# One attention score per key place modulo 128, later gate logits, and a planner that picks among sixty trial orders

## The chip, the core and the metric

The kernel runs on one core of a Trainium2 chip. The metric is device microseconds (us) of one execution, the median of several runs. A core has a matrix engine (TensorE, PE in the profile, with its weight loads shown as PEld), three engines for elementwise work (VectorE, DVE; ScalarE, ACT; GpSimd, POOL) and a queue of DMA issues (SyncE, SP). Matrix products land in PSUM, which VectorE and ScalarE read and GpSimd does not touch in this kernel.

## The reference

Attention with a window of 128 keys and a slope per head, then a mixture of eight experts whose gates are normalised in rounds over rows and columns, then one more two-layer network. Shapes: batch 4, 8 heads, 576 positions, head size 64; 2304 tokens of 512 features.

```python
def _attn_ref(q, k, v):
    window = 128
    scores = scale * np.matmul(q, k.transpose(0, 1, 3, 2))
    rel = pos[:, None] - pos[None, :]
    bias = slopes[:, None, None] * (-np.abs(rel))[None, :, :]
    mask = (rel >= 0) & (rel < window)
    scores = np.where(mask, scores + bias[None], -1000000000.0)
    scores = scores - np.max(scores, axis=-1, keepdims=True)
    attn = np.exp(scores)
    attn = attn / (np.sum(attn, axis=-1, keepdims=True) + 1e-09)
    return np.matmul(attn, v)
...
    x = _moe_ref(x=x, **moe_kwargs)      # logits, 8 rounds of row and column sums, 8 experts with relu
    return _moe2_ref(x=x, **moe2_kwargs) # x @ w_in, leaky relu, @ w_out
```

## The kernel before, in words

**Attention** walks 18 tiles of 128 tokens (`steps`, two groups of four heads each). A tile's queries can see keys of their own block and of the block before, so `scores` makes, per head, one product of 128 queries by 256 keys into PSUM (tile `s`, line 609). VectorE adds the slope times the distance, with a huge value where the window is left, and takes the minimum (line 618, 256 columns per head); ScalarE takes the exponential and its sum (line 622). `probs_T` turns the probabilities with TensorE, one 128x128 transpose per head and key block (line 690, tile `pt`), eight per group, and copies them out, half on ScalarE (line 693) and half on VectorE (line 695), as `pb`. `values` multiplies them with the values (line 708, tile `o`), and VectorE writes the weighted result into `acc` (line 716). The first tile of every second sequence (tiles 0 and 9) has no block before, so 16 tiles have two blocks. Sequences are 576 long, so tiles 4 and 13 hold the end of one and the start of the next, and tiles 5 and 14 stand 64 places into one; these four get a bias of their own (tile `dist`, line 575) and queries scaled on GpSimd (line 580).

**Inputs of the experts.** Each product of the experts is made by a scheme with seven block products, in pairs of 16-bit parts. `part` splits an input into a high part on ScalarE and a low part on GpSimd (`split`, lines 842 and 843); `sums` forms the block sums (line 894). Expert products of the first weight chunk (lines 1128 and 1244) run between attention's own products for the first pairs of tiles, and after it for the last. `logits` (line 736) makes the gate's logits of a pair of tiles, and `gate` the rounds.

**The order.** The program is written as one list, and `Plan` reorders it: `weigh` gives each instruction a cost in ns, `depend` finds what it waits for, `deadlines` works back from TensorE's products to the latest time that each instruction may end, and `order` fills the engines forward in time, at each step taking the ready instruction with the earliest latest time. `fix` ties each engine's instructions together in that order. TensorE products fall into three kinds (`mode`: by rows of 64 for the scores, by columns of 64 for values and sums, full for the rest), and `TURN` is the price of a change of kind. The order is a fixed one, made before the kernel runs.

```python
            near = t + (self.NEAR if eng != "PE" else 0)
            pick = min((i for i in at if at[i] <= near), key=lambda i: (latest[i], i))
```

## Time and profile before

| what | value |
|---|---|
| runs | 1840.07, 1840.01, 1834.02 us; median 1840.01 |
| the profiled execution | 1834.78 us, of which the span is 1833.0 |
| TensorE busy | 1807.0 us (99%), 17542 matmul records |
| VectorE, ScalarE, GpSimd busy | 1329.2 (73%), 1350.1 (74%), 1310.8 us (72%) |
| chain that ended last | TensorE 71% of the span; no other engine over 2% |
| granted TensorE clock | 0.997 of full speed on the mean |

Busy shares are means over the whole span. Matmuls are pipelined and their recorded durations overlap, so the distance between the starts of two neighbours tells what a product takes of TensorE's time; the same holds for short instructions of VectorE. A count such as "x8" in a timeline row joins neighbours of one line; a product of 32-bit numbers from 64 rows or 64 columns shows two records.

### The profile page before, as it was taken

To read this page: it belongs to the slowest core of one execution; us is meant where nothing else is said; L and a number is where in the kernel's file an instruction comes from. 1 tells how busy PE (TensorE), PEld (TensorE's weight loads), DVE (VectorE), ACT (ScalarE), POOL (GpSimd) and SP (SyncE) were. 2 spreads that over 40 slices of the span, in tenths; PEclk is the share of its full clock that TensorE was granted. 3 is DMA by queue.
4 is the path that set the end of the run, shared out by engine and by line. 5 is a ranking of instruction groups with operands and counts; after the bars stand their busy time and mean duration, and the time that the engine had idled before them with its cause. 6 is when DMAs were issued, how large, how long until landed. Compare 5 with 4: busy or idle time off the path is not lost.

```text
span 1833.0 us, 45057 instructions
## 1 busy us (share of the span) xinstructions
PE 1807.0 (99%) x17542; PEld 1603.2 (87%) x17542; DVE 1329.2 (73%) x3656; ACT 1350.1 (74%) x3099; POOL 1310.8 (72%) x1154
## 2 busy tenths in 40 slices
PE   8999999999999999999999999999999999999999
PEld 6677888889989898988989898989899888989888
DVE  6877677767777676777777667666666887777877
ACT  8989778767767767767767766667666789877664
POOL 3854778787869777787868777666766796776653
PEclk9999999999999999999999999999999999999999
DMA  8342020202112021202111120100001000101002
GB/s 292 106 130 75 2 82 30 87 19 82 53 47 67 34 73 39 87 19 81 53 47 54 46 82 6 43 24 24 24 24 48 1 25 24 47 2 47 2 33 73
DMA packets 61094, 97.80 MB, mean 53 GB/s; under 512 B 4560, under 2 KB 27600, under 8 KB 60880
## 3 DMA queue, kind: packets, MB, share of 16 engines
q1 hardware_dynamic: 60880, 94.93, 15.7%
q8 instruction: 137, 2.24, 0.5%
q14 instruction: 77, 0.63, 0.1%
HBM read 81.81 MB, written 13.11 MB: 52 GB/s over the span
## 4 chain that ended last, share of the span: by engine, by line
PE 71%; ACT 2%; DVE 2%; DMA 1%; POOL 1%; issue 0%; SPq 0%; ACTq 0%
PE t L1244 36%; PE s L1128 20%; PE sq L1128 15%; DMA raw<-in_moe_w_dram 1%; DVE sx L930 0%; DVE s L1156 0%; ACT acc L917 0%; POOL w L843 0%; ACT junk L976 0%; ACT h L1197 0%; PE xt L916 0%; POOL h L1200 0%; DVE acc L1257 0%; ACT raw L979 0%; ACT q L1140 0%
## 5 line engine op out<-in xcount | busy, mean ns | idle before, releaser
L1244 PE MATMUL t<-w,h 128*128 128x256 f16 x7560 | 949.3, 273 | 5.1 <-ACT acc L1251 3.2
L1128 PEld LDWEIGHTS <-w 128*128 128x128 f16 x8400 | 756.4, 98 | 89.3 <-issue 9.4
L1244 PEld LDWEIGHTS <-h 128*128 128x128 f16 x7560 | 735.1, 98 | 92.6 <-issue 7.5
L1128 PE MATMUL s<-xp,w 128*128 128x256 f16 (+1 forms) x4872 | 591.3, 262 | 2.6 <-ACT q L1140 1.3
L1257 DVE SCALAR_TENSOR_TENSOR acc<-t,pu,acc 128x256 f32<-128x256 f32 x866 | 406.6, 479 | 179.0 <-PE t L1244 151.0
L1200 POOL TENSOR_TENSOR h<-s,h 128x1024 f16<-128x1024 f32 x180 | 383.9, 2133 | 132.1 <-ACT h L1197 76.2
L1128 PE MATMUL sq<-xp,w 128*128 128x256 f16 (+1 forms) x3528 | 429.4, 262 | 1.9 <-DVE s L1156 1.1
L1255 POOL TENSOR_TENSOR acc<-acc,part 128x256 f32<-128x256 f32 x322 | 234.3, 729 | 194.3 <-ACT part L1254 75.7
L843 POOL TENSOR_TENSOR w<-raw,w 128x512 f16<-128x512 f32 x240 | 274.9, 1162 | 46.6 <-ACT w L842 46.4
L1140 ACT ACTIVATE q<-s 128x256 f32<-128x256 f32 x364 | 138.9, 382 | 135.9 <-PE s L1128 133.2
L1197 ACT ACTIVATE h<-s 128x1024 f16<-128x1024 f32 x180 | 190.1, 1056 | 47.0 <-DVE s L1156 45.5
L1156 DVE SCALAR_TENSOR_TENSOR h<-sq,h 128x512 f16<-128x512 f32 x352 | 193.0, 553 | 30.5 <-ACT h L1175 24.4
L1254 ACT ACTIVATE part<-t,pu 128x256 f32<-128x256 f32 x322 | 151.7, 471 | 76.3 <-PE t L1244 71.6
L1144 DVE SCALAR_TENSOR_TENSOR sq<-s,q 128x256 f32<-128x256 f32 x176 | 75.9, 431 | 149.1 <-PE s L1128 91.9
L1144 DVE SCALAR_TENSOR_TENSOR sq<-sq,q 128x256 f32<-128x256 f32 x352 | 150.2, 427 | 37.7 <-PE sq L1128 34.3
L842 ACT ACTIVATE w<-raw 128x512 f16<-128x512 f32 x240 | 148.1, 631 | 12.3 <-PE s L1128 3.9
L1156 DVE SCALAR_TENSOR_TENSOR s<-sq,s 128x256 f32<-128x256 f32 x352 | 146.1, 415 | 0.7
L1175 ACT ACTIVATE h<-sq 128x512 f16<-128x512 f32 x176 | 104.7, 595 | 56.2 <-DVE sq L1144 47.1
L1156 DVE SCALAR_TENSOR_TENSOR s<-sq,q 128x256 f32<-128x256 f32 x352 | 136.7, 417 | 10.6 <-ACT q L1152 8.8
L976 ACT ACTIVATE junk<-raw 128x512 bf16<-128x512 f32 x160 | 100.8, 630 | 11.9 <-DMA raw<-in_moe_w_dram 8.4
L979 ACT ACTIVATE raw<-raw,sr 128x512 f32<-128x512 f32 x160 | 108.4, 719 | 0.1
L1003 POOL TENSOR_TENSOR raw<-raw 128x512 f32<-128x512 f32 x80 | 102.0, 1275 | 0.4 <-DVE dg L819 0.4
(151 smaller groups left out, 1643.1 us busy)
## 6 DMA issues: line engine op xcount, KB each, us to landing
raw<-in_moe_w_dram SPq DMA_DIRECT2D x32, 768.0 KB, 4.7
k_t<-in_k_dram SPq DMA_DIRECT2D x16, 512.0 KB, 4.1
raw<-in_moe_w_dram SPq DMA_DIRECT2D x32, 256.0 KB, 3.6
raw<-in_moe_w_in_dram SPq DMA_DIRECT2D x16, 512.0 KB, 3.6
raw<-in_moe_w_out_dram SPq DMA_DIRECT2D x16, 512.0 KB, 3.5
q_t<-in_q_dram SPq DMA_DIRECT2D x18, 256.0 KB, 3.0
acc<-in_v_dram SPq DMA_DIRECT2D x18, 256.0 KB, 6.0
v_t<-in_v_dram SPq DMA_DIRECT2D x18, 256.0 KB, 2.9
```

The lines of the kernel that those rows point to most:

```text
L842: nc.scalar.activation(out=hi, in_=src, func=AF.Copy)
L843: return nc.gpsimd.tensor_tensor(out=lo, in0=src, in1=hi, op=ALU.subtract)
L1128: nc.tensor.matmul(d[b][:, f, :], t[:, wp, kk, ft * P:(ft + 1) * P], XP[p][:, o, kk, xp, :], start=(i == 0 and f == 0 and j in FIRST), sto ...
L1140: nc.scalar.activation(out=q[:, k], in_=ps, func=AF.Copy, scale=CS)
L1144: nc.vector.scalar_tensor_tensor(out=block(k), in0=ps, scalar=CS, in1=q[:, k], op0=ALU.mult, op1=ALU.add)
L1156: nc.vector.scalar_tensor_tensor(out=out, in0=in0, scalar=sc, in1=in1, op0=op0, op1=op)
L1197: nc.scalar.activation(out=h[:, 3:7, 0, :], in_=d["s"], func=AF.Copy)
L1200: nc.gpsimd.tensor_tensor(out=h[:, 3:7, 1, :], in0=d["s"], in1=h[:, 3:7, 0, :], op=ALU.subtract)
L1244: nc.tensor.matmul(ps, h[:, o, hp, f, tt * P:(tt + 1) * P], w[:, wp, ft, :], start=(i == 0 and j in FIRST), stop=(i == 5), skip_group_chec ...
L1254: nc.scalar.activation(out=part, in_=ps, func=AF.Copy, scale=s)
L1255: nc.gpsimd.tensor_tensor(out=dst, in0=dst, in1=part, op=ALU.add)
L1257: nc.vector.scalar_tensor_tensor(out=dst, in0=ps, scalar=s, in1=dst, op0=ALU.mult, op1=ALU.add)
```

## The change

- **Scores.** The score product stays at 256 keys. Where a tile has a block before, `copy_predicated` then overwrites, in PSUM, each own-block score whose key lies ahead of the query by the score of the key 128 places earlier: within a window of 128, exactly one of the two counts. Softmax runs over 128 columns. Tiles 0, 4, 5, 9, 13 and 14 get extra masking instructions (`drop`) in place of their own bias and scaled queries.
- **Probabilities.** One transpose per head, four per group, into one tile. The own block's part is the product with a mask on VectorE (`own`); the part of the block before is a copy on ScalarE, from which a select on GpSimd then removes the rest.
- **Setup.** The masks `ahead`, `own` and `other` and a distance of 128 columns replace the 256-column distance; the slopes have 128 columns per head.
- **Logits** of pairs 3 and 4 move from before the gate's list to places inside it, beside the expert products.
- **The planner** gets other constants, a price for selects, a price for DMA issues, dependencies between engines on one PSUM tile, a bias against changes of kind, a slow clock for the first 11.5 us, and `best`: sixty trials, in each of which a tenth of the latest times is moved at random; the trial with the least TensorE idle time up to 260 us, by the planner's own prices, is taken.

```diff
+    HORIZON = 260e3
+    TRIALS = 60
+    SHIFT = 2000.0
...
         elif eng == "Pool":
-            node["cost"] += 190 + 1.89 * n if "float16" in kinds else 185 + 2.12 * n
+            if kind not in ("InstTensorTensor", "InstTensorCopy"):
+                node["cost"] += 187 + 0.84 * n
+            else:
+                node["cost"] += 190 + 1.89 * n if "float16" in kinds else 185 + 2.12 * n
...
-            pick = min((i for i in at if at[i] <= near), key=lambda i: (latest[i], i))
+            turn = 20 if eng == "PE" else 0
+            pick = min((i for i in at if at[i] <= near),
+                       key=lambda i: (latest[i] + turn * self.TURN.get((mode, nodes[i]["mode"]), 0), i))
...
+    def best(self, latest):
+
+        chance = random.Random(1)
+        self.order(latest, self.HORIZON)
+        least = self.lost
+        moved = [i for i, node in enumerate(self.nodes) if self.starts[i] > 0 and node["eng"] != "SP"]
+        for _ in range(self.TRIALS):
+            other = list(latest)
+            for i in chance.sample(moved, len(moved) // 10):
+                other[i] += chance.gauss(0, self.SHIFT)
+            self.order(other, self.HORIZON)
+            if self.lost <= least:
+                latest, least = other, self.lost
+        return self.order(latest)
...
+    def drop(x, mask):
+        nc.vector.scalar_tensor_tensor(out=x, in0=spread(mask, x.shape[2]), scalar=-BIG, in1=x, op0=ALU.mult, op1=ALU.add)
...
         for r in range(2):
+            mine = s[r][:, :, P:2 * P]
+            if at:
+                nc.vector.copy_predicated(mine, spread(ahead, P).bitcast(I32), s[r][:, :, 0:P])
+            if at == 0:
+                drop(mine, ahead)
+            elif S - P < at:
+                drop(mine[64:128], other[64:128])
+            elif at < P:
+                drop(mine[0:64, :, 0:64], ahead[0:64, 0:64])
             for n in range(2):
                 h = 4 * quad + 2 * n + r
...
                 nc.vector.tensor_tensor_reduce(
-                    out=e[r][:, n, 0:W], in0=s[r][:, n, 0:W], in1=bias[:, c0:], scale=scale,
+                    out=e[r][:, n], in0=mine[:, n], in1=slopes[:, h], scale=-0.125,
                     scalar=float(2**41), op0=ALU.add, op1=ALU.min, accum_out=mn[:, 2 * n + r:2 * n + r + 1],
                 )
...
     def probs_T(i, quad):
         c = st[i][quad]
...
+        pt = new(ps_t, [P, 4, P], F32, tag="pt", name="pt")
         for r in range(2):
...
             for n in range(2):
-                for b in range(nb):
-                    ins = nc.tensor.transpose(pt[:, n, b, :], c["e"][r][:, n, b * P:(b + 1) * P], ident)
...
+                nc.tensor.transpose(pt[:, 2 * r + n, :], c["e"][r][:, n], ident)
+        part = [None, None]
+        for b in range(2 - len(st[i]["kb"]), 2):
+            pb = part[b] = new(ap3, [P, 4, P], F32, tag=f"pb{b}", bufs=2, name="pb")
+            if b == 0:
+                nc.scalar.activation(out=pb, in_=pt, func=AF.Copy)
+                nc.gpsimd.affine_select(out=pb, in_=pb, pattern=[[0, 4], [-1, P]], base=0, channel_multiplier=1,
+                                        compare_op=ALU.is_gt, fill=0.0)
             else:
-                nc.vector.tensor_copy(pb[:, :, 0:nb, :], pt[:, :, 0:nb, :])
...
+                nc.vector.tensor_tensor(out=pb, in0=pt, in1=own.unsqueeze(1).to_broadcast([P, 4, P]), op=ALU.mult)
...
-    for p in (3, 4):
-        logits(p)
-        tick()
-    gating += [None] * 16 + gate()
+    gating += [None] * 8 + [lambda: logits(3), None, lambda: logits(4)] + [None] * 5 + gate()
```

**What moves: TensorE, late in attention.** Line 609 (638 in the change) is the score product, 690 (720) the transposes, 708 (742) the values, 664 (697) and 678 (711) small products for the softmax sums, 823 (857) one for a scale. Before:

```order
L609 MATMUL s<-k_t,q_t 128x256 x4
L690 MATMUL pt<-ident,e 128x128 x8
L708 MATMUL o<-pb,v_t 64x128 x8
L690 MATMUL pt<-ident,e 128x128 x4
L609 MATMUL s<-k_t,q_t 128x256 x4
L690 MATMUL pt<-ident,e 128x128 x4
L664 LDWEIGHTS pieces
L664 MATMUL rt<-identb,pieces 112x128
L708 MATMUL o<-pb,v_t 64x128 x8
```

Now:

```order
L742 MATMUL o<-pb,v_t 64x128 x16
L720 MATMUL pt<-ident,e 128x128 x4
L638 MATMUL s<-k_t,q_t 128x256 x4
L742 MATMUL o<-pb,v_t 64x128 x16
L697 LDWEIGHTS pieces
L697 MATMUL rt<-identb,pieces 112x128
L720 MATMUL pt<-ident,e 128x128 x4
L857 LDWEIGHTS ones
L857 MATMUL mt<-dg,ones 128x128
L638 MATMUL s<-k_t,q_t 128x256 x4
```

A group has one stretch of four transposes instead of two, and the values of two groups stand together.

**VectorE, early in attention.** Line 618 (652) is the score reduction, whose second row reads out its minimum; 695 and 729 make the turned probabilities; 643 is the predicated copy; 649 (682) the reciprocal of the sums. Before:

```order
L649 RECIPROCAL sm<-sm 128x8
L618 ISA e,mn<-s,slopes 128x256
L618 ISA mn 128x1
...
L695 COPY pb<-pt 128x512
L716 SCALAR_TENSOR_TENSOR acc_99<-o,srx,rb 128x512
```

Now:

```order
L729 TENSOR_TENSOR pb<-pt,own 128x512
L643 COPY_PREDICATED s<-ahead,s 128x2x128
L682 RECIPROCAL sm<-sm 128x8
L652 ISA e,mn<-s,slopes 128x128
L652 ISA mn 128x1
L643 COPY_PREDICATED s<-ahead,s 128x2x128
```

Four reductions of 256 columns became two predicated copies and four reductions of 128.

**ScalarE, behind attention.** Line 842 (876) makes the high parts of the inputs of pairs 3 and 4, line 1251 (1285) writes out an expert product that TensorE's next one waits for, 1140 (1174) and 1175 (1209) belong to the first expert layer. Before:

```order
L680 ACTIVATE rb<-rt 128x512
L842 ACTIVATE xp_2803<-acc_110 128x4x128
L842 ACTIVATE xp_2803<-acc_112 128x2x128
L842 ACTIVATE xp_2803<-sx 128x8x128
L842 ACTIVATE xp_2803<-acc_111 128x4x128
L842 ACTIVATE xp_2803<-acc_113 128x2x128
L842 ACTIVATE xp_2803<-sx 128x8x128
L842 ACTIVATE xp_2804<-acc_114 128x4x128
L842 ACTIVATE xp_2804<-acc_115 128x2x128
L842 ACTIVATE xp_2804<-h 128x8x128
L1251 ACTIVATE acc_102<-t_2945,pu 128x256
```

Now:

```order
L713 ACTIVATE rb<-rt 128x512
L876 ACTIVATE xp_2729<-acc_109 128x4x128
L876 ACTIVATE xp_2729<-acc_111 128x2x128
L876 ACTIVATE xp_2729<-sx 128x8x128
L876 ACTIVATE xp_2729<-acc_110 128x4x128
L876 ACTIVATE xp_2729<-acc_112 128x2x128
L876 ACTIVATE xp_2730<-acc_113 128x4x128
L1285 ACTIVATE acc_101<-t_2801,pu 128x256
L876 ACTIVATE xp_2730<-acc_114 128x2x128
L1209 ACTIVATE h<-sq 128x2x256
L876 ACTIVATE xp_2729<-sx 128x8x128
L1285 ACTIVATE acc_101<-t_2801,pu 128x256
```

Three of the nine splits now stand behind the first write-out.

## Rows read from the trace of the kernel before

**Rows 1.** Busy time by stretch (columns: us, PE, PEld, DVE, ACT, POOL, clock, DMA).
```profile
20.00:176.40 156.40, 150.67 (x1592) 117.24 (x1591) 122.96 (x457) 145.24 (x452) 84.17 (x99) 0.98 0.43 138
40.00:60.00 20.00, 17.17 (x150) 12.14 (x146) 16.38 (x69) 19.38 (x59) 15.30 (x16) 0.92 0.36 109
60.00:80.00 20.00, 18.55 (x186) 14.68 (x185) 14.49 (x48) 18.45 (x55) 17.43 (x17) 0.99 0.43 133
80.00:100.00 20.00, 19.60 (x232) 15.77 (x230) 15.62 (x52) 18.43 (x55) 16.09 (x19) 1.00 0.46 145
...
400.00:600.00 200.00, 199.85 (x1956) 180.34 (x1954) 143.19 (x368) 142.58 (x309) 157.37 (x134) 1.00 0.19 59
```

**Rows 2.** Timeline of TensorE: attention's last values product, and the first expert wait behind.
```profile
175.35 1.09 PE L708 MATMUL o<-pb,v_t 128*64 128x128 f32 x16
...
183.23 2.71 PE L1244 MATMUL t<-w,h 128*128 128x256 f16 x12 [2.94 <-ACT acc L1251]
```

**Rows 3.** Timeline of TensorE inside attention (start, us, line, operation, tiles, count).
```profile
156.25 0.66 PE L690 MATMUL pt<-ident,e 128*128 128x128 f32 x4
156.84 1.09 PE L708 MATMUL o<-pb,v_t 128*64 128x128 f32 x16
...
162.58 1.09 PE L690 MATMUL pt<-ident,e 128*128 128x128 f32 x8
163.60 1.09 PE L708 MATMUL o<-pb,v_t 128*64 128x128 f32 x16
```

**Rows 4.** Timeline of VectorE: reductions of 128 and of 256 columns, PSUM instruction.
```profile
5.92 0.29 DVE L618 CUSTOM_DVE_ANT_0 e<-s,slopes 128x128 f32<-128x128 f32 x1 [4.78 <-PE s L609]
...
6.14 0.29 DVE L618 CUSTOM_DVE_ANT_0 e<-s,slopes 128x128 f32<-128x128 f32 x1
...
159.62 0.42 DVE L618 CUSTOM_DVE_ANT_0 e<-s,slopes 128x256 f32<-128x256 f32 x1 [0.30 <-PE s L609]
...
159.97 0.42 DVE L618 CUSTOM_DVE_ANT_0 e<-s,slopes 128x256 f32<-128x256 f32 x1
...
175.31 0.43 DVE L1144 SCALAR_TENSOR_TENSOR sq<-sq,q 128x256 f32<-128x256 f32 x1 [0.20 <-ACT junk L976]
175.65 0.15 DVE L814 TENSOR_REDUCE m<-mxw 128x1 f32<-128x4 f32 x1
```

**Rows 5.** Groups by line and shape, 0 to 280 us: busy us, mean ns, idle before.
```profile
L622 ACT ACTIVATE e<-e,mn 128x256 f32<-128x256 f32 x128 | 63.6, 499 | 2.9 <-DVE mn L618 2.3
...
L618 DVE CUSTOM_DVE_ANT_0 e<-s,slopes 128x256 f32<-128x256 f32 x96 | 36.3, 421 | 12.5 <-PE s L609 8.0 <-PE pt L690 3.6 <-ACT sm L647 0.8
...
L1144 DVE SCALAR_TENSOR_TENSOR sq<-sq,q 128x256 f32<-128x256 f32 x21 | 8.9, 426 | 2.7 <-PE sq L1128 2.1 <-ACT junk L976 0.2
...
L622 ACT ACTIVATE e<-e,mn 128x128 f32<-128x128 f32 x16 | 6.2, 393 | 0.2 <-DVE mn L618 0.2
...
L618 DVE CUSTOM_DVE_ANT_0 e<-s,slopes 128x128 f32<-128x128 f32 x16 | 3.9, 289 | 8.1 <-PE s L609 7.5 <-PE pt L690 0.5
...
L637 POOL TENSOR_SCALAR_AFFINE_SELECT sel<-sel 128x512 bf16<-128x512 bf16 x3 | 2.0, 667 | 0.2
...
L549 POOL TENSOR_SCALAR_AFFINE_SELECT e<-e 128x256 f32<-128x256 f32 x1 | 0.4, 401 | 0.1
...
L843 POOL TENSOR_TENSOR xp<-sx,xp 128x1024 f16<-128x1024 f32 x8 | 17.1, 2134 | 1.0 <-ACT xp L842 1.0
```

**Rows 6.** Timeline of ScalarE behind attention: first and last piece of the splits.
```profile
177.39 0.94 ACT L842 ACTIVATE xp<-acc 128x512 f16<-128x512 f32 x2 [1.34 <-DVE acc L716]
...
182.73 0.81 ACT L1251 ACTIVATE acc<-t,pu 128x256 f32<-128x256 f32 x2
```

More of the change, by code (lines that the diff above doesn't have):

```diff
@@ L1 @@
 import heapq
+import random
 from contextlib import ExitStack
@@ L44 @@
     FROM_PE = 203
-    LANDING = 2000.0
-    PER_NS = 350.0
+    LANDING = 2250.0
+    FIRST = 740.0
+    PAUSE = 1200.0
+    COLD = 11500.0
     NEAR = 60.0
@@ L132, in weigh @@
         if "DMA" in kind:
-            sizes = [x[1][0][1] * x[4] * x[3] for x in reads + writes if x[0].split("_")[0] != "in"]
-            node["cost"], node["landing"] = max(sizes) / self.PER_NS, self.LANDING
+            size, row = max((x[1][0][1] * x[4] * x[3], x[1][-1][1] * x[3]) for x in reads + writes if x[0][:3] != "in_")
+            node["cost"] = max(size / (390.0 if row != 1024 else 290.0), 480.0)
+            node["landing"] = self.LANDING
         elif eng == "PE":
@@ L226, in depend @@
                         found.add(k)
+                    elif mask and name in self.whole and self.nodes[k]["eng"] != node["eng"]:
+                        found.add(k)
                     if mask & ~w:
@@ L276, in deadlines, with order @@
         return latest
-    def order(self, latest):
+    def order(self, latest, until=float("inf")):
         nodes, behind = self.nodes, self.behind
@@ L293, in order @@
         self.turns = []
-        lag = 0.0
+        lag, work = 0.0, 0.0
         def since(i):
@@ L311, in takes @@
             if node["eng"] == "PE":
-                cost += self.TURN.get((mode, node["mode"]), 0)
+                cost += self.TURN.get((mode, node["mode"]), 0) + (0.9 * cost if t < self.COLD else 0)
             elif node["shared"] and gpsimd[0] <= t < gpsimd[1]:
@@ L357, in order @@
             end = start + cost
+            if eng == "SP" and len(orders["SP"]) == 1:
+                end += self.PAUSE
             if eng == "PE":
                 mode = node["mode"]
+                work += node["cost"]
+                self.lost = end - work
+                if end > until:
+                    return None
                 lag = max(lag, end - self.ends[pick])
@@ L370, in order @@
             free[eng] = end - (self.START[eng] if cost > 100 else 0)
+            end = start + cost
             waiting[eng].remove(pick)
@@ L407, in fix @@
         products = [i for i, node in enumerate(self.nodes) if node["eng"] == "PE"]
-        for picks in self.order(self.deadlines(products)).values():
+        for picks in self.best(self.deadlines(products)).values():
             line = [ins for i in picks for ins in self.nodes[i]["ins"]]
@@ L442, in attn_moe_kernel @@
     HF = FC // 2
-    BIG = float(2**40)
+    BIG = float(2**43)
     EPS = 1e-9
@@ L486, in attn_moe_kernel @@
     wg = new(const, [P, KT, E], F32, name="wg")
-    qscale = new(const, [P, NP], F32, name="qscale")
     Pm = new(const, [P, NTILE, E], F32, name="Pm")
@@ L500, in attn_moe_kernel @@
     wout32 = new(dram, [F2, DM], F32, name="wout32")
-    for h in range(H):
-        r = 64 * (h % 2)
-        nc.gpsimd.memset(qscale[r:r + 64, h // 2:h // 2 + 1], -(D ** -0.5) * 2.0 ** (8.0 * (h + 1) / H))
     side, gating, inputs = [], [], []
@@ L544, in attn_moe_kernel @@
     ps_o = actx.enter_context(tc.tile_pool(name="ps_o", bufs=1, space=PSUM))
-    ramp = new(ap1, [P, 2, 2 * P], F32, tag="e", bufs=4, name="e")
-    dist = ramp[:, 0]
-    nc.gpsimd.iota(dist, pattern=[[-1, 2 * P]], base=P, channel_multiplier=1, allow_small_or_imprecise_dtypes=True)
-    nc.gpsimd.affine_select(out=dist, in_=dist, pattern=[[1, 2 * P]], base=0, channel_multiplier=-1,
-                            compare_op=ALU.is_gt, fill=BIG)
-    nc.gpsimd.affine_select(out=dist, in_=dist, pattern=[[-1, 2 * P]], base=P, channel_multiplier=1,
-                            compare_op=ALU.is_ge, fill=BIG)
-    slopes = new(ap1, [P, H, 2 * P], F32, name="slopes")
+    ahead = new(ap1, [P, P], F32, name="ahead")
+    nc.gpsimd.memset(ahead, 1.0)
+    nc.gpsimd.affine_select(out=ahead, in_=ahead, pattern=[[1, P]], base=0, channel_multiplier=-1,
+                            compare_op=ALU.is_gt, fill=0.0)
+    dist = new(ap1, [P, P], F32, name="dist")
+    nc.gpsimd.iota(dist, pattern=[[-1, P]], base=0, channel_multiplier=1, allow_small_or_imprecise_dtypes=True)
+    nc.vector.scalar_tensor_tensor(out=dist, in0=ahead, scalar=float(P), in1=dist, op0=ALU.mult, op1=ALU.add)
+    slopes = new(ap1, [P, H, P], F32, name="slopes")
     for h in range(H):
         nc.scalar.activation(out=slopes[:, h], in_=dist, func=AF.Copy, scale=-8.0 * 2.0 ** (-8.0 * (h + 1) / H))
+    own = new(ap1, [P, P], F32, name="own")
+    nc.vector.tensor_tensor(out=own, in0=ahead, in1=ident, op=ALU.add)
+    other = new(ap1, [P, P], F32, name="other")
+    nc.vector.tensor_copy(other, ahead)
+    nc.vector.memset(other[64:128, 0:64], 1.0)
     qv = qT.rearrange("(a p) t -> p a t", p=P)
@@ L603, in scores @@
         s = [new(ps_s, [P, 2, 2 * P], F32, tag="s", name="s") for _ in range(2)]
-        e = [new(ap1, [P, 2, 2 * P], F32, tag="e", bufs=4, name="e") for _ in range(2)]
+        e = [new(ap1, [P, 2, P], F32, tag="e", bufs=6, name="e") for _ in range(2)]
         c[quad] = dict(e=e)
```

49 lines of the change are left out of this document (15 added, 34 removed).

## The prediction, as it was put on record

> **What bounds the kernel now.** I first read the busy time of each engine by stretch. In a stretch of the expert products TensorE is busy 199.85 of 200 us [rows 1], so whatever shortens the kernel must take work or idle time from TensorE, and the place to look is the one where it is not full: attention. The matmul timeline shows where that ends: the last values product starts at 175.35 us and takes 1.09 [rows 2], so attention ends at 176.4 us. From 20 to 176.4 us [rows 1] TensorE is busy 150.67 of 156.4 us (96%), ScalarE 145.24 (93%), VectorE 122.96 (79%) and GpSimd 84.17 (54%). The reader is to see that three engines are nearly equally loaded here: taking work from TensorE alone is worth only what the other two let through. Behind attention stands one more hole, 2.94 us before the expert product at 183.23 us, waiting for ScalarE [rows 2].
>
> The profiled execution took 1834.78 us, 5.2 below the median of the runs (1840.01) and 0.8 above the lowest. The sum below is made against it. About 0.5%, 9.2 us, is what a measurement of this kernel can tell from no change.
>
> **The change, part by part.**
>
> *Transposes.* With one score per key place, a group of four heads has 4 transposes instead of 8. Sixteen of the 18 token tiles have two key blocks and two groups each, so 32 x 4 = 128 transposes go. Price: between a score product and a values product, four transposes take 0.59 us (156.25 to 156.84) and eight take 1.02 (162.58 to 163.60) [rows 3], so four are 0.43, one 0.1075, and 128 are 13.8 us of TensorE. What is left of the 0.59 is 0.16 for two changes of product kind, 0.08 each. By the order, TensorE changes kind 109 times instead of 136 in the whole program: 27 x 0.08 = 2.2 us. Before the end of attention the order has 288 expert products instead of 282, six more at about 0.11 (the 12 at 183.23 took 2.71 at the low clock, half of that at the full one [rows 2]): +0.65, which is gone from the part behind. TensorE from 20 us on: 150.67 - 13.8 - 2.2 + 0.65 = 135.3 us.
>
> *Softmax on ScalarE.* 128 exponentials have 128 columns instead of 256: 128 x (499 - 393 ns) = 13.6 us less [rows 5]. The probability copies stay at one of 512 columns per two-block group. ScalarE: 145.24 - 13.6 = 131.6 us.
>
> *VectorE.* This is the part that pays. Prices are distances between starts, since the next instruction starts before the last has quite ended [rows 4]: a score reduction of 256 columns 0.35 (159.62 to 159.97), one of 128 columns 0.22 (5.92 to 6.14), and an instruction that reads and writes PSUM over 256 columns 0.34 (175.31 to 175.65).
> - 128 reductions shrink: -128 x 0.13 = -16.6.
> - 64 predicated copies are added (two per two-block group). The trace has none. The nearest row is the 256-column instruction from PSUM into PSUM, with a mask in place of its second operand: 0.34, so +21.8. Bounds: 0.22, as if it cost no more than 128 columns (14.1), and 0.68, as if it passed twice, once for the mask and once for the data (43.5). A gain is excluded, as the instruction is added and removes nothing. I take 0.34, because its columns and its memory are those of the row.
> - 24 masking instructions on the first and the crossing tiles: 16 x 0.34 + 8 x 0.22 = +7.2, of which four (1.4) fall before 20 us.
> - The probability piece for the own block is one product with a mask per group, 36 of 512 columns, where 32 copies of 512 and four of 256 stood: the four longer ones cost 4 x 256 columns at (0.35 - 0.22)/128, +1.0.
> - Four small setup instructions, under 0.22 each, +0.9, before 20 us.
>
> Net +14.3, of which +12.0 behind 20 us: 122.96 + 12.0 = 135.0 us. VectorE now is as full as TensorE. With the bounds of the predicated copy it would be 127.3 or 156.8.
>
> The Trainium skill ("VectorE: DVE Perf Modes", Rules for kernel authors) speaks against this change: every VectorE instruction pays its pipeline drain, so one is to keep the number of instructions low, and this change adds 88 inside attention. By that rule each instruction would cost its whole duration. The rows disagree, since starts are 0.34 to 0.35 apart where durations are 0.42 [rows 4, 5]; the rule's sum stands among the rivals.
>
> *GpSimd.* 32 selects of 512 columns are new, one behind each ScalarE copy of probabilities. Bounds: 0.667 us, the mean of the 512-element select on 16-bit data, and 0.80, twice the 256-column one of 0.401 [rows 5]. At 0.667 they are 21 us over 156, beside 84: the engine stays at two thirds on average, so I cost the engine at nothing. The cover is TensorE's other work between a group's transposes and its values product; if it is gone, each select's own length and the wait for its turn appear (a rival below). Four scalings of q and their memsets leave GpSimd, which I count as slack.
>
> *The seam behind attention.* Before, nine splits of inputs stood in one row on ScalarE, from 177.39 to the evacuation at 182.73 us [rows 6], 5.3 us, and TensorE waited for that evacuation. The new order puts three of the nine (256, 1024 and 1024 of 5376 columns, 43%, 2.3 us) behind the first evacuation. GpSimd's part of the same splits is late next, so I count 1.3 of the 2.94 us as won. The later logits of the last two pairs move no work, only its place.
>
> *The planner.* Sixty trials choose an order with less idle TensorE by the planner's own prices. That buys no work; it decides how tightly the engines are packed, which is the next step. The first 20 us and everything behind 200 us I leave as they are: there TensorE is full or waits for the first loads, the first eight of which stand in the same order.
>
> **The sum.** From 20 us on the needs are now 135.3 (TensorE), 135.0 (VectorE) and 131.6 (ScalarE), instead of one engine ahead at 150.67. Packing: ScalarE, which had to keep up, ran at 93% beside a TensorE at 96%. With three equal engines I take 93%: 135.3 / 0.93 = 145.5, so attention ends at 165.5 us instead of 176.4: 10.9 us. With 0.65 for the six products and 1.3 for the seam it is 12.9 us, so 1821.9 at the level of the profiled execution and 1827.1 at that of the median. I put **1824** between them. Packed at 89% the gain is 6.3, at 96% it is 17.9; that is the forecast's own range.
>
> **The rivals.**
> 1. *Everything packs.* At 100% attention ends at 155.3 us, the gain is 23.1 and the time 1811.7. For it: the new order has half as many groups of transposes to place, and the planner now searches. Against it: no stretch of attention has had three full engines.
> 2. *GpSimd becomes the bound in the middle.* From 40 to 100 us it is busy 48.8 of 60 us [rows 1]; 12 of the 32 selects fall there by share, 8.2 us, which is 57 of a stretch that should itself shrink to 56. A select waits behind splits of up to 2.13 us [rows 5], so on the mean half of that plus its own length, 1.7 us; 12 x 1.7 = 21 us, and if TensorE's look-ahead hides only half, 10.7 us are lost: 1832.6. For it: the values product needs the select. Against it: over the whole of attention the engine is a third idle, and the order can put selects ahead of splits.
> 3. *VectorE instructions do not overlap.* Then the copies cost 64 x 0.426, the masking 16 x 0.426 + 8 x 0.289 and the reductions save 128 x 0.132: +18.8 behind 20 us, 141.8 us, attention ends at 172.5, and with the two us above the gain is 5.9: 1829. The rule of the skill named above says this; starts in rows 4 speak against it.
> 4. *The predicated copy passes twice (slower).* At 0.68 us VectorE needs 156.8 us, at 93% attention ends at 188.6, 12.2 late; less 2.0 for seam and products it is +10.2, 1845. It decides from 0.53 us per copy on (no gain), and makes it slower by 9.2 from 0.67 on. For it: the destination keeps old values, so it may have to be read. Against it: a three-operand instruction over the same columns takes 0.34.
>
> That the change does not do what it says can only concern the planner: the order does lose the transposes and the changes of kind, but an order that is better by the planner's prices may be no better on the chip. That is the low end of the packing, inside the forecast's range.
>
> **How the numbers follow.** Forecast 0.62, of which 0.12 gain less than 9.2 us (packing under 91%); everything packs 0.10; GpSimd 0.16; no overlap 0.03; slower copy 0.09. Faster by over 0.5%: 0.50 + 0.10 = 0.60. Within: 0.12 + 0.16 + 0.03 = 0.31. Slower: 0.09. The range is 1811 to 1838: from the fully packed case at the lower level to the GpSimd case at the level of the median; the slow copy stays outside.
>
> **What would show it.** Right: 144 transposes instead of 272; predicated copies near 0.34 apart; the last values product ending near 165 us; VectorE over 90% busy from 20 us to there; a wait under 2 us behind it; the rest shifted as a block. Wrong: copies at 0.6 or more; TensorE waiting for GpSimd's selects between 40 and 100 us; or an attention that ends early with a hole behind it as long as the gain.

## The result, and the profile after

The changed kernel takes **1816.49 us** (median of 4 runs, 1815.33 to 1822.00) beside 1837.31 us for the kernel before (4 runs, 1834.02 to 1840.07): a ratio over all runs of **0.9894**, 95% interval 0.9869 to 0.992 (the two medians alone give 0.9887). That is inside the range of the prediction, near its low end, 7.5 us under the predicted 1824. The profiled execution took 1816.0 us (span 1814.3), 18.8 less than that of before, which is just past the 17.9 of the forecast's own tightest packing.

I split the span where the last values product ends (start 167.74 us, 1.09 long). TensorE's timeline, the rows that this part uses:

```profile
40.26 1.87 PE L638 MATMUL s<-k_t,q_t 64*128 64x256 f32 x8 [1.40 <-DVE mn L652]
...
43.61 2.46 PE L638 MATMUL s<-k_t,q_t 64*128 64x256 f32 x8 [0.44 <-DVE mn L652]
46.01 0.29 PE L857 MATMUL mt<-dg,ones 128*128 128x128 bf16 x1
...
54.82 1.13 PE L638 MATMUL s<-k_t,q_t 64*128 64x256 f32 x8
55.89 0.66 PE L720 MATMUL pt<-ident,e 128*128 128x128 f32 x4
...
81.34 0.71 PE L638 MATMUL s<-k_t,q_t 64*128 64x128 f32 x6 [1.62 <-DVE mn L652]
...
130.72 0.27 PE L697 MATMUL rt<-identb,pieces 128*112 128x128 bf16 x1 [2.71 <-DVE pb L729]
...
167.74 1.09 PE L742 MATMUL o<-pb,v_t 128*64 128x128 f32 x16
...
173.43 3.56 PE L1278 MATMUL t<-w,h 128*128 128x256 f16 x30 [0.82 <-DVE k L859]
```

So attention ends at 168.8 us instead of 176.4 [rows 2]: **7.6 us**. Behind it stand 1645.5 us instead of 1656.6: **11.1 us**. More than half of the gain lies where the prediction counted 2. The wait of 2.94 us behind attention [rows 2] has become one of 0.82, for VectorE.

The same windows as [rows 1], and two more behind attention (columns: us, PE, PEld, DVE, ACT, POOL, clock, DMA), of the changed kernel:

```profile
20.00:168.83 148.83, 140.26 (x1460) 110.97 (x1461) 129.60 (x534) 128.61 (x443) 99.78 (x123) 0.92 0.46 148
40.00:60.00 20.00, 18.16 (x127) 12.86 (x128) 16.25 (x85) 16.83 (x62) 19.16 (x19) 0.74 0.45 145
60.00:80.00 20.00, 19.71 (x238) 15.96 (x235) 18.63 (x77) 18.55 (x61) 12.01 (x16) 1.00 0.51 158
80.00:100.00 20.00, 18.66 (x181) 15.75 (x183) 18.09 (x60) 18.36 (x64) 18.20 (x22) 0.91 0.46 145
...
168.83:208.83 40.00, 39.00 (x420) 34.58 (x419) 31.79 (x96) 33.76 (x76) 34.66 (x31) 1.00 0.01 2
400.00:600.00 200.00, 199.68 (x1952) 179.90 (x1950) 144.81 (x376) 146.37 (x320) 154.60 (x132) 1.00 0.20 62
1381.30:1581.30 200.00, 199.93 (x1956) 180.72 (x1954) 158.22 (x436) 165.68 (x375) 151.81 (x121) 1.00 0.08 28
```

and of the kernel before, the 40 us behind attention and the stretch from 433 to 233 us before the end, which answer to two of these:

```profile
176.44:216.44 40.00, 35.76 (x359) 30.57 (x359) 25.28 (x81) 28.77 (x63) 29.51 (x26) 0.96 0.01 2
1400.00:1600.00 200.00, 195.83 (x1906) 175.76 (x1904) 156.04 (x431) 162.76 (x363) 150.21 (x119) 1.00 0.08 26
```

Two things are to be seen. TensorE's idle time behind attention went from 4.24 to 1.00 us in the first stretch and from 4.17 to 0.07 in the second. And inside attention the granted clock fell from 0.98 to 0.92: in two long stretches, from 41 and from 130 us, and a short one from 82 us, TensorE ran at the lower level (1.2 GHz). The four score products of a group (eight records) take 2.40 us there (43.61 to 46.01), against 1.07 at the full clock (54.82 to 55.89).

The groups that answer to [rows 5], by line and shape, 0 to 200 us (busy us, mean ns, idle before), and what TensorE waits for from 20 to 182 us:

```profile
L652 DVE CUSTOM_DVE_ANT_0 e<-s,slopes 128x128 f32<-128x128 f32 x144 | 34.1, 285 | 0.9 <-PE pt L720 0.2
L643 DVE COPY_PREDICATED s<-ahead,s 128x256 f32<-128x256 int32 x64 | 24.8, 425 | 10.6 <-PE s L638 10.1
L729 DVE TENSOR_TENSOR pb<-pt,own 128x512 f32<-128x512 f32 x36 | 24.7, 685 | 4.0 <-ACT pb L725 3.3 <-PE o L742 0.2
L656 ACT ACTIVATE e<-e,mn 128x128 f32<-128x128 f32 x144 | 56.1, 392 | 10.9 <-DVE mn L652 10.7
L726 POOL TENSOR_SCALAR_AFFINE_SELECT pb<-pb 128x512 f32<-128x512 f32 x32 | 21.1, 661 | 42.8 <-ACT pb L725 32.3 <-DVE dg L853 6.8 <-DVE sx L928 3.1
```

```profile
PE s L638 <- DVE mn L652: 4.1, 4, 1.6
PE rt L697 <- DVE pb L729: 2.7, 1, 2.7
PE s L638 <- issue: 1.1, 1, 1.1
PE t L1278 <- DVE k L859: 0.8, 1, 0.8
...
PE o L742 <- POOL pb L726: 0.2, 1, 0.2
```

In attention TensorE now waits mostly for VectorE, hardly for GpSimd. The new instruction on VectorE's timeline answers to [rows 4]:

```profile
101.04 0.76 DVE L643 COPY_PREDICATED s<-ahead,s 128x256 f32<-128x256 int32 x2 [0.23 <-PE s L638]
101.71 0.28 DVE L652 CUSTOM_DVE_ANT_0 e<-s,slopes 128x128 f32<-128x128 f32 x1
...
101.92 0.28 DVE L652 CUSTOM_DVE_ANT_0 e<-s,slopes 128x128 f32<-128x128 f32 x1
```

Two predicated copies fill 101.04 to 101.71: 0.335 us each, and a reduction 0.21 (forecast 0.34 and 0.22). The Trainium skill's rule ("VectorE: DVE Perf Modes", Rules for kernel authors) is to keep the number of instructions low, since a pipeline drain follows each. As the prediction read it, each copy would have cost its whole duration, 0.425; that does not show here.

On ScalarE behind attention, answering to [rows 6], six of the nine splits (2, 1 and 3 in the rows) stand ahead of the first write-out, which starts 3.1 us after the first split instead of 5.3:

```profile
169.79 0.94 ACT L876 ACTIVATE xp<-acc 128x512 f16<-128x512 f32 x2 [1.29 <-DVE acc L750]
170.63 1.04 ACT L876 ACTIVATE xp<-sx 128x1024 f16<-128x1024 f32 x1
171.58 1.44 ACT L876 ACTIVATE xp<-acc 128x512 f16<-128x512 f32 x3
172.92 0.45 ACT L1285 ACTIVATE acc<-t,pu 128x256 f32<-128x256 f32 x1
```

### The profile page after: what moved, and what is told of

The parts are those of the page before. It is cut to its first block, busy times and chain, and to the rows that moved or that the text cites. A ratio compares the mean times of both kernels' runs of the same rounds, so it can differ in the third digit from the quotient of the medians.

```text
span 1814.3 us, 44994 instructions
## 1 busy us (share of the span) xinstructions
PE 1793.6 (99%) x17414; PEld 1596.6 (88%) x17414; DVE 1340.3 (74%) x3748; ACT 1329.8 (73%) x3091; POOL 1326.0 (73%) x1170
## 4 chain that ended last, share of the span: by engine, by line
PE 90%; DMA 3%; DVE 3%; POOL 2%; ACT 1%; issue 1%; SPq 0%; DVEq 0%; POOLq 0%; ACTq 0%
PE t L1278 43%; PE s L1162 25%; PE sq L1162 18%; PE s L638 2%; PE o L742 1%; DMA raw<-in_moe_w_dram 1%; PE pt L720 1%; POOL w L877 1%; DMA raw<-in_moe_w_in_dram 1%; DMA raw<-in_moe_w_out_dram 0%; PE xt L950 0%; POOL raw L1115 0%; DMA wg<-in_moe_w_gate_dram 0%; ACT junk L1010 0%; POOL raw L1111 0%
```

## The experiments

Each kernel is the one before or the changed one with the edit shown; any edit makes the planner draw up the whole order anew, so a row differs from its neighbour by the edit and by another draw of the order. The table gives the ratio to the kernel before on the same chip, and from each profile: the end of attention (start and duration of its last values product), and TensorE's idle time (stretch less busy) in the 40 us behind it, from there to 433 us before the end ("middle"), and from 433 to 233 us before the end ("late").

| kernel | ratio (interval) | attention ends | 40 us | middle | late |
|---|---|---|---|---|---|
| before | 1 | 176.4 | 4.2 | 1.5 | 4.2 |
| before, dependency alone | 0.9971 (0.9961–0.9982) | 176.7 | 4.1 | 5.7 | 1.6 |
| before, late logits alone | 0.9971 (0.9958–0.9983) | 176.1 | 0.9 | 3.1 | 4.2 |
| old attention and logits, new planner | 0.9936 (0.992–0.9953) | 170.1 | 4.7 | 2.3 | 1.7 |
| old attention, new planner, late logits | 0.9943 (0.9928–0.9959) | 175.6 | 0.9 | 2.4 | 0.5 |
| new attention, old planner with dependency | 0.9938 (0.9922–0.9955) | 174.9 | 1.4 | 1.2 | 0.1 |
| changed, early logits | 0.9915 (0.99–0.993) | 166.5 | 3.7 | 4.0 | 0.1 |
| changed, no trials | 0.9896 (0.9881–0.9911) | 168.5 | 1.7 | 2.8 | 0.3 |
| changed, old constants | 0.9902 (0.9887–0.9917) | 165.3 | 2.3 | 4.7 | 0.2 |
| changed, copies twice | 0.9949 (0.9935–0.9964) | 178.2 | 2.7 | 2.3 | 0.3 |
| changed, selects twice | 0.993 (0.9914–0.9947) | 173.5 | 2.8 | 3.1 | 0.5 |
| changed, trials judged to the end | 0.9901 (0.9887–0.9916) | 169.3 | 2.0 | 2.1 | 0.0 |
| the same, other seed | 0.9927 (0.9912–0.9942) | 167.8 | 3.5 | 7.0 | 0.5 |
| changed | 0.9894 (0.9869–0.992) | 168.8 | 1.0 | 1.1 | 0.1 |

### First four: which half brings the gain

My theory was that the shorter end of attention comes from the transposes and that the planner does the rest; the rivals, that the order alone brings all, or that the holes behind depend on when attention ends.

Old attention and logits with the whole new planner (the class `Plan` of the changed kernel in the kernel before):

> The attention and the early logits of the kernel before, with the whole planner of the change (constants, prices, dependency between engines on one PSUM tile, bias against changes of kind, sixty trials). Theory 'work': what attention gained (its end moved from 176.4 to 168.8 us) comes from the 128 transposes and the shorter softmax, the rest (11 us behind attention) from the planner; then here attention ends at 174 to 177 us, the hole of 4.2 us at 1400 to 1600 us is gone, and the time is 1823 to 1828 at the level of the profiled runs. Rival 'planner': the order alone brings nearly all; then attention ends before 171 us and the time is 1815 to 1820. Rival 'phase': the holes behind attention come and go with the moment at which attention ends, whatever the planner; then the time stays within 3 us of before.

New attention and late logits with the old planner, which keeps of the new one the dependency between engines alone (the new attention without it was not tried):

```diff
+                    elif mask and name in self.whole and self.nodes[k]["eng"] != node["eng"]:
+                        found.add(k)
```

> The attention and logits of the change with the planner of before, to which only the dependency between engines on one PSUM tile is added. Theory 'work': attention ends at 168 to 172 us, the seam and the hole at 1400 to 1600 us stay as before, time 1825 to 1830. Rival 'planner': attention ends at 174 us or later, because selects are priced at twice their length and nothing searches; time 1832 or more. Rival 'phase': the hole at 1400 to 1600 us changes by over 2 us here too.

The changed kernel without trials:

```diff
-    TRIALS = 60
+    TRIALS = 0
```

> The change with no trials (one order, all other parts of the planner kept). Theory 'work': the trials are worth at most 3 us, all of it before 260 us: attention ends at 169 to 172 us, time 1816 to 1820. Rival 'planner': without the search attention ends at 174 us or later and the time is 1823 or more.

The changed kernel with the old prices of DMAs and of the start:

```diff
-    LANDING = 2250.0
+    LANDING = 2000.0
...
-            node["cost"] = max(size / (390.0 if row != 1024 else 290.0), 480.0)
+            node["cost"] = size / 350.0
...
-        free["SP"] = self.FIRST
...
-            if eng == "SP" and len(orders["SP"]) == 1:
-                end += self.PAUSE
...
-                cost += self.TURN.get((mode, node["mode"]), 0) + (0.9 * cost if t < self.COLD else 0)
+                cost += self.TURN.get((mode, node["mode"]), 0)
```

> The change with the old landing time and price of a DMA and without the slow clock, the first issue and the pause at the start; trials, bias, dependency and select price kept. Theory 'work' says nothing of these; if they are what closed the hole at 1400 to 1600 us (a load that lands later than planned), the hole of about 4 us is back and the time is 1820 to 1823; if the hole stays closed, it was the dependency or the bias. Rival 'phase': attention's end moves by over 2 us and the hole comes back only if it does.

My theory came out the wrong way round for the end of attention. The new planner alone moves attention's end by 6.3 us and leaves the 40 us behind it as they were; the new attention with the late logits moves the end by only 1.5 and the part behind by 10.5 (1656.6 to 1646.1). In neither did one theory hold whole: attention ends as the rival 'planner' says in both, but the time of the first (1826.6 us in the profiled execution) is what 'work' says, and that of the second (1825.6) is under the 1832 of 'planner'. Attention's rows with the planner alone, then with the new attention alone:

```profile
20.00:170.11 150.11, 146.85 (x1571) 116.59 (x1571) 117.96 (x456) 140.55 (x445) 83.24 (x99) 0.99 0.45 147
```

```profile
20.00:174.93 154.93, 141.59 (x1466) 110.23 (x1467) 135.81 (x546) 130.15 (x444) 99.92 (x124) 0.93 0.45 144
```

The old attention is packed to 98% (146.85 of 150.11) at a clock of 0.99. The new one has 5.3 us less TensorE time but is packed to 91%, at 0.93: what the transposes free is lost in waits and at the lower clock. In time the two halves are equal (0.9936 and 0.9938; both hold the dependency), and the changed kernel has about both. What the new attention is worth beside the new planner, two pairs of the table tell that differ in it alone: with early logits it moves attention's end from 170.1 to 166.5 us and the ratio from 0.9936 to 0.9915, with late ones from 175.6 to 168.8 us and from 0.9943 to 0.9894. That is 3.6 and 6.8 us at the end of attention; the intervals of the first pair overlap.

The trials are worth nothing that this measurement can tell (0.9896 against 0.9894). With the old constants attention ends 3.5 us earlier at a clock of 0.98, and loses 7.0 behind it:

```profile
20.00:165.31 145.31, 138.15 (x1480) 107.89 (x1479) 131.29 (x551) 130.94 (x455) 98.46 (x124) 0.98 0.49 157
205.31:1384.80 1179.49, 1174.79 (x11358) 1057.18 (x11356) 830.17 (x2161) 841.26 (x1827) 899.91 (x768) 1.00 0.15 48
```

### Next: what closed the holes behind attention

The dependency between engines alone (the two lines shown above, in the kernel before):

> The kernel before, whose planner gets one thing of the change: a TensorE, VectorE or ScalarE instruction on a shared PSUM tile now follows earlier ones of another engine on that tile, as the chip makes it wait anyway. Asked: what closed the stretch of 1400 to 1600 us, where TensorE of the kernel before was idle 4.17 of 200 us and in all variants with the new planner or the new attention between 0.07 and 1.7. Theory 'dependency': the old planner did not see these waits and placed work where it could not start; then the same stretch (433 to 233 us from the end) is idle under 1 us, attention still ends within 1.5 us of 176.4, the 40 us behind it stay idle 4 us, and the time is 0.995 to 0.999 of before. Rival 'phase': the stretch depends on when attention ends and on which products are left over, not on the dependency; then its idle time stays at 3 us or more while attention ends where it did, and the ratio is 0.999 to 1.002.

The changed kernel with the logits early:

```diff
-    gating += [None] * 8 + [lambda: logits(3), None, lambda: logits(4)] + [None] * 5 + gate()
+    for p in (3, 4):
+        logits(p)
+        tick()
+    gating += [None] * 16 + gate()
```

> The changed kernel with the logits of pairs 3 and 4 put back ahead of the gate's list. Asked: what closed the gap behind attention, where TensorE of the kernel before was idle 4.2 of 40 us at a granted clock of 0.96 and in the changed kernel 1.0 at 1.00. Theory 'logits': the early logits put work between attention and the inputs of pairs 3 and 4; put back, the 40 us behind attention are idle 3 us or more, the clock there falls to 0.96 to 0.98, the time behind attention rises from 1645.5 to 1649 us or more, and the ratio to before is 0.991 to 0.993 instead of 0.989. Rival 'lighter attention': with fewer ScalarE columns and fewer transposes left over, the inputs are ready sooner whatever the logits do; then the 40 us stay idle under 2 us, the clock at 1.00, and the ratio is 0.988 to 0.991.

The kernel before with the late logits alone (the same lines, the other way):

> The kernel before with one thing of the change, the later logits of pairs 3 and 4. Theory 'logits stand alone': attention ends where it did (176.4 within 1.5 us), the 40 us behind it lose at least half of their 4.2 idle us, and the time behind attention falls by 3 to 8 us: ratio 0.995 to 0.998. Rival 'not with the old order': the inputs of pairs 3 and 4 stand in one row on ScalarE as before, TensorE waits 2.9 us for the write-out behind them, and the ratio is 0.999 to 1.001.

Old attention, new planner and late logits:

> The attention of the kernel before with the whole new planner and the later logits of pairs 3 and 4: the change without its score and probability part. With the early logits this attention gave 0.9936 of before (0.992 to 0.9953), attention ending at 170.1 us and 1654.7 us behind it. Theory 'logits stand alone': placing them beside the expert products frees the start of the part behind attention whatever attention looks like; then the part behind takes 1645 to 1650 us, the 40 us behind attention are idle under 2 us, and the ratio is 0.988 to 0.991, as in the changed kernel: the new scores would be worth nothing by themselves. Rival 'only together': with the old attention the inputs of pairs 3 and 4 are late because ScalarE and VectorE are still full at its end; then the 40 us stay idle 3 us or more at a clock under 1.00, and the ratio is 0.992 to 0.995.

**The late logits narrow the gap behind attention.** Three pairs differ in them alone, and in all three the 40 us tell the same: idle 4.2 to 0.9 us (old planner, old attention), 4.7 to 0.9 (new planner, old attention), 3.7 to 1.0 (new planner, new attention), and the clock there goes from 0.96 to 1.00 each time. In the kernel before with the late logits alone, ScalarE's and TensorE's rows show how:

```profile
177.07 0.94 ACT L842 ACTIVATE xp<-acc 128x512 f16<-128x512 f32 x2 [2.01 <-DVE acc L716]
...
180.64 0.61 ACT L842 ACTIVATE xp<-acc 128x512 f16<-128x512 f32 x1
181.16 0.45 ACT L1251 ACTIVATE acc<-t,pu 128x256 f32<-128x256 f32 x1
```

```profile
181.66 1.47 PE L1244 MATMUL t<-w,h 128*128 128x256 f16 x12 [0.80 <-ACT acc L1251]
```

The write-out that TensorE waits for starts at 181.16 us, with splits still behind it, instead of at 182.73 behind all nine [rows 6]; TensorE waits 0.80 us instead of 2.94, and its next 12 products take 1.47 us at the full clock instead of 2.71 at the lower one [rows 2]. By the planner's code, and not by a run, the reason is that a split is due when the logits that read it are due: late logits make the splits less urgent than the write-out. What the pairs gave in all differs, because the order in front moved too: 0.29% for the kernel before, 0.2% with intervals that overlap for the changed one, nothing for the old attention with the new planner, whose attention ended 5.5 us later in exchange. In the first two kernels the theory held by every figure. In the last it held by the 40 us and the part behind (1647.2 us), but not by the ratio: the changed kernel, with the new scores, is faster.

They do not close the gap in every order. The four kernels with early logits are idle 3.7 to 4.7 us in the 40 us, the ten with late ones 0.9 to 3.5. With the instructions of the changed kernel TensorE waits 1.5 to 2.1 us for the write-out again in the four other orders (no trials, old constants, and the two judged to the end), in three of them with the clock at 0.96; the other seed:

```profile
167.77:207.77 40.00, 36.51 (x371) 31.90 (x372) 29.00 (x86) 30.19 (x67) 29.56 (x26) 0.96 0.01 2
```

So in the changed kernel most of the step from 3.7 to 1.0 us can be the draw; the two pairs with the old attention are one draw on each side.

**The dependency closes the late hole.** The two kernels without it are idle 4.2 us there, the twelve with it between 0.0 and 1.7. Rows of the late stretch, with the dependency alone and with the late logits alone:

```profile
216.66:1400.70 1184.04, 1178.32 (x11384) 1059.82 (x11383) 829.79 (x2164) 841.85 (x1826) 901.57 (x768) 1.00 0.15 48
1400.70:1600.70 200.00, 198.45 (x1938) 179.18 (x1938) 158.34 (x436) 165.62 (x374) 150.77 (x120) 1.00 0.08 27
```

```profile
1396.60:1596.60 200.00, 195.84 (x1905) 175.76 (x1904) 155.45 (x428) 162.40 (x360) 150.21 (x119) 1.00 0.08 27
```

By the end of attention, the 40 us and the ratio the theory held, though 1.6 us stay idle where I expected under 1. But what the dependency closes late it need not win: the middle of the same kernel, upper row, is idle 5.7 us where that of before is idle 1.5, so that behind attention TensorE is idle 15.0 us in all instead of 13.1, and the profiled execution (1835.47 us, the longest of its ten runs, which begin at 1828.61) is no shorter than that of before. Most of what makes these runs differ goes with the clock: five with a mean granted clock of 0.999 or 1.000 take 1828.6 to 1830.7 us, four with 0.997 take 1834.5 to 1835.2. The profiled one, at 0.999, does not fit, and why stays open. The rival 'phase', by which the holes follow the moment when attention ends, is not needed here: with the dependency alone and with the late logits alone that moment moves by 0.3 us or less, and each changes another hole.

### VectorE and GpSimd loaded further

Each predicated copy done twice:

```diff
                 nc.vector.copy_predicated(mine, spread(ahead, P).bitcast(I32), s[r][:, :, 0:P])
+                nc.vector.copy_predicated(mine, spread(ahead, P).bitcast(I32), s[r][:, :, 0:P])
```

> The changed kernel with each of the 64 predicated copies done twice in a row (the second one changes nothing); the planner plans with them. This adds 64 x 0.37 = 23.7 us to VectorE, which is busy 129.6 us of the 148.8 between 20 us and the end of attention. Theory 'VectorE bounds attention': at the same busy share of 87% attention takes 176 us from 20 us on and ends near 196 instead of 168.8, ratio to before 1.003 to 1.006. Rival 'VectorE has slack': TensorE waits for VectorE only 8 us in attention, so the copies fill its idle time first; VectorE goes to 95% or more, attention ends at 175 to 182, ratio 0.992 to 0.997. No effect (attention ends before 172) would mean that neither engine's sum matters and only the low granted clock does.

Each select done twice:

```diff
                 nc.gpsimd.affine_select(out=pb, in_=pb, pattern=[[0, 4], [-1, P]], base=0, channel_multiplier=1,
                                         compare_op=ALU.is_gt, fill=0.0)
+                nc.gpsimd.affine_select(out=pb, in_=pb, pattern=[[0, 4], [-1, P]], base=0, channel_multiplier=1,
+                                        compare_op=ALU.is_gt, fill=0.0)
```

> The changed kernel with each of the 32 selects on GpSimd done twice in a row (the second one changes nothing). This adds 32 x 0.66 = 21.1 us to GpSimd, busy 99.8 of 148.8 us between 20 us and the end of attention. Theory 'GpSimd is covered': TensorE has other work between a group's transposes and its values product; attention ends within 2.5 us of 168.8, ratio to before 0.988 to 0.991. Rival 'GpSimd is near the bound in the middle': the selects stand behind input splits, TensorE waits for them between 40 and 100 us, attention ends at 174 or later, ratio 0.993 or more.

Attention with the copies doubled, then with the selects doubled:

```profile
20.00:178.20 158.20, 141.74 (x1468) 110.81 (x1464) 146.55 (x602) 130.20 (x449) 97.84 (x124) 0.95 0.44 140
```

```profile
20.00:173.53 153.53, 139.27 (x1462) 108.89 (x1462) 133.43 (x546) 129.57 (x443) 119.02 (x154) 0.96 0.46 146
```

With 64 copies more, VectorE is busy 146.55 of 158.2 us (93%), attention ends 9.4 us later and the time rises by half a per cent. Of the 21.4 us that 64 copies take by the distance of their starts, the end of attention shows under half, so VectorE in the changed kernel had slack; TensorE now waits 9.9 us for reductions instead of 4.1. The rival's end of attention and ratio held, its 95% did not. Doubled selects end attention 4.7 us later, between the two theories, while TensorE waits only 1.0 us for selects; 0.993 is also what another draw of the order gives (0.9927, below). So this one is inconclusive.

### Choosing the order better

```diff
-    HORIZON = 260e3
+    HORIZON = float("inf")
```

> The changed kernel, whose sixty trials are judged by TensorE's idle time over the whole program instead of up to 260 us. Behind attention the variants so far are idle 5.5 us (the changed kernel) to 15 us, mostly in waits of 0.3 to 1.1 us for ScalarE at 400 to 1000 us, with no order by when attention ends. Theory 'the planner can see them': judged to the end, the trials pick an order with fewer of them; idle time behind attention under 5 us, ratio 0.985 to 0.988, a kernel faster than the changed one. Rival 'they are below its prices': waits this short hang on durations that the planner does not know so closely; ratio 0.988 to 0.992, idle time behind attention 5 to 10 us.

and with `random.Random(3)` in place of `random.Random(1)`:

> The same, with the trials drawn from another random seed. Asked: how much of the time is the draw. Theory 'the draw does not matter': within 2 us of the other seed, both for the end of attention and for the idle time behind it. Rival 'accident': the two differ by more than 3 us in the end of attention or in the idle time behind, as the variants so far did (attention's end 165.3 to 168.8 for the same instructions under slightly different prices).

No gain: 0.9901 and 0.9927. The two differ by the seed alone, and by 6.4 us of idle time behind attention (14.2 against 7.8, with the end stretch); the second is idle 7.0 us in the middle:

```profile
207.77:1391.50 1183.73, 1176.78 (x11366) 1057.92 (x11364) 820.16 (x2163) 836.75 (x1825) 897.83 (x767) 1.00 0.15 48
```

So the draw is worth some 0.3%: the five kernels with the instructions of the changed one lie between 0.9894 and 0.9927. A difference of that size between two rows of the table is therefore not shown to be the edit's. The changed kernel has the least idle time behind attention of all fourteen. No version beat it.

## Why the prediction was right, and where not

- **The total** was right partly by compensation and partly by luck: in the profiled executions 18.8 us against 12.9. Attention gave less than forecast (7.6 against 10.9), the part behind far more (11.1 against 2.0). The luck is the draw: in the profiles of the five kernels with the same instructions the part behind takes 1645.5 to 1656.7 us, against 1656.6 before, and the changed kernel has the shortest.
- **Prices: right.** Predicated copies 0.335 us (taken 0.34, bounds 0.22 and 0.68), reductions 0.21 (0.22), selects 0.661 (0.667), exponentials 392 ns (393), 144 transposes. The case of copies that pass twice and that of no overlap fell with the first two.
- **Attention: the mechanism right, TensorE's time mis-sized.** The forecast was 135.3 / 0.93 = 145.5 us from 20 us on; measured are 140.3 us of work in 148.8. The packing, 94%, is about what was taken; TensorE's time is 5.0 us over its term. What was missing is the clock. At a mean of 0.92 some 24 us of attention ran at the lower level (before, at 0.98, some 6), so at half speed up to 12 us against 3 went to it: up to 9 more, which covers the 5.0. The three dips stand behind idle TensorE: a wait of 1.40 us for VectorE until 40.26 us, with shorter ones after it, one of 1.62 until 81.34 and one of 2.71 until 130.72 us. With the clock at 0.98 (old constants) attention ended at 165.3, where the forecast had put it; in the other four kernels with these instructions, at 0.92 to 0.94, it ended at 167.8 to 169.3. No run changes the clock alone. That VectorE would be as full as TensorE was also too high: 129.6 us for 135.0, and 87% from 20 us on, not 93. The new scores are worth less than the sum of the forecast says: 3.6 and 6.8 us at the end of attention in the two pairs that differ in them alone, where 10.9 was forecast, and the planner moves the end of the old attention by 6.3 without them.
- **"Everything behind 200 us I leave as they are": wrong.** The late hole, 4.2 us in the trace of the kernel before, was left out; the dependency between engines, two lines of the change that the prediction did not cost, closes most of it by itself (1.6 us stay). What keeps the middle as full as before (1.1 us idle, against 5.7 with the dependency alone and 7.0 with another seed) is not shown.
- **"The later logits move no work, only its place" and the 1.3 us for the seam: the failed step.** The reordered splits were seen, but put down to the new order and sized from the wait alone. In the kernel before the late logits by themselves bring them about, and the seam of the changed kernel gives 3.2 us of idle time and the time at the lower clock behind it, 1.24 us for the first 12 products alone. Of the 11.1 us behind attention 7.6 are idle time (13.1 to 5.5, with the end stretch); the other 3.5 are TensorE's own time, of which the clock of the 40 us explains 1.6 (0.96 of 40 us is 3.2 us at half speed), the six products that moved ahead 0.65 by the prediction's price, and the rest was not traced.
- **Rivals.** *Everything packs* did not come: TensorE is busy 140.3 of 148.8 us, though the profiled 1816.0 us is nearer to its 1811.7 than to the forecast's 1821.9. *GpSimd in the middle* did not come either: it is busy 49.4 of 60 us from 40 to 100, where this case had counted 57 of 56, and TensorE waits 0.2 us for selects.
- **The planner** "buys no work": true, but with the old attention its order is worth 0.64% by itself, as much as the new attention with the late logits; its trials are worth nothing measurable.

## What to carry to other kernels

A small consumer's place sets when its feeders are due: the logits of two pairs of tiles, moved later, let a write-out pass part of a row of splits, and in each of three pairs narrowed the gap behind it, though another order of the same instructions opens it again. Taking work from the fullest of three nearly full engines gives back only part of it, since the others then make it wait, and in the changed kernel three waits of 1.4 to 2.7 us on TensorE were followed by three to ten microseconds at half its clock. And where a planner redraws the whole order after any edit, compare several draws first: here they differ by 0.3%, as much as the dependency or the late logits alone are worth.

## Unexpected on the hardware

The lower clock inside attention. Rows of the changed kernel in steps of 2 us:

```profile
128.00:130.00 2.00, 0.00 (x1) 0.13 (x1) 2.00 (x10) 1.98 (x7) 1.92 (x5) 1.00 0.11 38
130.00:132.00 2.00, 1.28 (x6) 1.09 (x7) 1.96 (x11) 1.91 (x10) 2.00 (x2) 0.53 0.00 0
132.00:134.00 2.00, 2.00 (x12) 1.35 (x10) 1.25 (x6) 0.15 (x1) 2.00 (x5) 0.50 0.00 0
...
138.00:140.00 2.00, 2.00 (x18) 1.40 (x16) 1.11 (x5) 0.00 (x0) 0.00 (x0) 0.50 0.03 8
140.00:142.00 2.00, 2.00 (x28) 1.78 (x26) 1.70 (x8) 1.74 (x3) 0.75 (x2) 0.91 0.03 8
```

TensorE idles 2.7 us, and when it works again the granted clock is 0.50, and it stays there for some ten microseconds in which TensorE is not idle again. The wait itself is about a third of its price: at half the clock those ten microseconds do the work of five, so five are lost beside the 2.7.

Not every wait is followed by this. Behind attention TensorE waits for the same write-out in the kernel before, 2.94 us until 183.23 [rows 2], and in the kernel with the dependency alone, 2.93 us. The clock falls in the first and not in the second, whose next 12 products take 1.47 us instead of 2.71. The row of the second kernel's timeline, then 184 to 186 us of the kernel before and of the second:

```profile
183.46 1.47 PE L1246 MATMUL t<-w,h 128*128 128x256 f16 x12 [2.93 <-ACT acc L1253]
```

```profile
184.00:186.00 2.00, 2.00 (x12) 1.36 (x10) 0.28 (x1) 0.91 (x3) 2.00 (x2) 0.50 0.00 0
```

```profile
184.00:186.00 2.00, 2.00 (x21) 1.79 (x19) 0.43 (x1) 2.00 (x6) 2.00 (x2) 1.00 0.00 0
```

What decides between the two is not shown. Runs of one kernel differ as well: the ten with the dependency alone have mean granted clocks of 0.997 to 1.000, so the order of the instructions alone does not fix the clock.
